# A sliding-window and a linear attention block in one kernel: six units fewer in the first superblock, and a new order of the filling work

## The chip, the cores and the metric

The kernel runs on one core of a Trainium2 chip. The metric is device time in microseconds (us) of one execution. Three runs of the kernel before gave 305.0, 306.4 and 856.78; their median is 306.4. A further execution was recorded by the hardware profiler; every duration of single instructions below is from it.

The core's engines work in parallel, each through its own instructions in order: TensorE (PE; its weight loads are shown as PEld), VectorE (DVE), ScalarE (ACT), GpSimd (POOL) and SyncE (SP, which here only issues transfers). Matrix products land in PSUM banks, from which VectorE or ScalarE must take them ("evacuate") before a bank can be used again.

## What is computed

Two independent attention blocks, A and B, each with its own input of 2048 rows by 640, 32 heads of width 20, an input projection (640 by 1920) and an output projection (640 by 640). Their results stand side by side in the output. All tensors are bf16.

```python
def A(x, wqkv, wo):                      # causal softmax attention in a window of 256
    q, k, v = heads_of(x @ wqkv)
    scores = einsum("bhqd,bhkd->bhqk", q, k) * 20 ** -0.5
    scores = where((i_q - i_k >= 0) & (i_q - i_k < 256), scores, -1e9)
    return merge(einsum("bhqk,bhkd->bhqd", softmax(scores), v)) @ wo

def B(x, wqkv, wo):                      # linear attention, not causal
    q, k, v = heads_of(x @ wqkv)
    phi = lambda t: where(t > 0, t + 1, exp(t)) + 1e-6
    kv = einsum("bhsd,bhse->bhde", phi(k), v)      # one 20 x 20 matrix a head
    z = einsum("bhsd->bhd", phi(k))
    num = einsum("bhqd,bhde->bhqe", phi(q), kv)
    return merge(num / (einsum("bhqd,bhd->bhq", phi(q), z)[..., None] + 1e-6)) @ wo
```

## The kernel before

**Superblocks, groups and units.** The 2048 rows are cut into four superblocks (`s`) of 512 rows, each of four blocks of 128. The 32 heads make eight groups (`g`) of four. For A, a query block meets its own key block (masked along the diagonal, kind "D"), the one before it (whole, "F") and the one before that (masked at the edge of the window, "E"). The table `TILES` lays these blocks for one superblock and group into three tiles, each four block columns wide; a tile of one group is a **unit**, so there are 4 x 8 x 3 = 96. Key blocks ahead of the first row don't exist, so in the first superblock the first tile has three block columns, the second two and the third four.

**One unit.** `scores` (L429) multiplies queries and keys of four heads at once into S_ps, which takes four PSUM banks and has a single buffer; ScalarE takes the exponential of the used columns into the tile p, of which there are three (L439); GpSimd masks the D and E blocks in p (`affine_select`, L455). Two units later (`LAG = 2`) `values` (L476) multiplies p with the values into O_ps, one PSUM bank with a single buffer. The values carry a column of ones, so the sum of the weights comes out beside them. After a group's third tile VectorE takes the reciprocal (L489) and the product (L490) into otok, a tile of one buffer, which four transposing transfers turn into oT for the output projection (L501).

**The filling work.** Everything else is one long sequence of generators, `fill`. Each yields the number of columns after every matrix product; the main loop emits a unit, then takes from `fill` until a credit of (`FILL` - `TAIL`) / units = 345680 / 96 = 3601 columns is used up. 17920 columns (`EARLY`) are taken ahead of the first unit, and some 22000 are left for the end. So the order of `fill` and the credit fix, in the program, what stands between two units on every engine. The parts of `fill`, all through a pool of three PSUM banks named dense (`dps`):

- `a_qk(s)` projects A's queries and keys, 25600 columns. VectorE evacuates into st (L165), and `bounce` writes st to scratch in memory (L198) and at once reads it back from there into qpad or kpad, heads apart (four transfers on SP's queue, L201).
- `a_v(s)`: A's values, 12800 columns (L173, evacuated at L165).
- `b_kv(s)`, 28800 columns: `tok_rows` projects B's keys, five chains, each followed by `phi` (ScalarE's exponential into e at L181 or L297, then two VectorE instructions at L182 or L298, the clamp, and L185 or L306); then `v_proj`, eight chains of values; then phi(k) times v into kv_acc (L320, L328, L330). In the last superblock kv_acc is multiplied with bd, a mask of ones where a row belongs to its own head, into kv_bd (L334). `build_masks` makes bd at the start.
- `b_q(s)`: phi of B's queries, five chains, 12800 columns.
- `b_num(s)`: eight halves, two to a block of rows; three products (L382), then on VectorE the sum + 1e-6 (L391), its reciprocal (L394) and the product (L395) into otokB, then a transposing transfer (L404). A half counts as 450 columns.
- `a_out(s)`, `b_out(s)`: the output projections, five chains each, evacuated into osb (L165); GpSimd issues the store (L282).
- `load`: a transposing transfer of 512 input rows into xA or xB (two buffers each), on SP's queue (L98).

`alt(a, b)` takes one yield of a, then five of b, in turn. The order before is

```python
fill = seq(a_qk(1), a_v(1), load("A", 2), b_kv(0), load("B", 2), b_kv(1), load("B", 3),
    a_qk(2), a_v(2), load("A", 3), a_out(0), b_kv(2), load("B", NS), b_kv(3), load("B", NS + 1),
    a_qk(3), a_v(3), b_q(0), load("B", NS + 2), alt(b_num(0), seq(a_out(1), b_q(1))), load("B", NS + 3),
    alt(b_num(1), seq(b_out(0), b_q(2))), alt(b_num(2), seq(b_out(1), b_q(3))),
    alt(b_num(3), a_out(2)), b_out(2), b_out(3))
```

Ahead of it stand `a_qk(0)`, the loads of B's first two superblocks and `a_v(0)`; behind it `a_out_last`, the last output projection of A. With the first unit `late_loads` issues three weight loads on GpSimd.

## Time and profile before

| what | us |
|---|---|
| median of three runs | 306.4 |
| the profiled execution | 306.14 |
| its span, first to last instruction | 304.4 |
| TensorE, matrix products busy | 275.2 |
| ScalarE busy | 193.8 |
| VectorE busy | 184.7 |
| GpSimd busy | 163.3 |
| exponentials of p (L439), 96 | 170.1 |
| masks of p (L455), 184 | 146.7 |

The first scores start at 33.83, the first exponential of p at 36.60, the last one at 283.47; the last evacuation begins at 301.2. So 37 us go before the units and 19 behind the last exponential. The granted TensorE clock is full throughout.

How to read the lines: in a timeline a line has the start and the length in us, the engine, the line of the kernel, the operation, output<-inputs with their shape, how often (x), and in brackets how long the engine had been idle before it and what released it. A list of groups has the busy time, the mean in ns, and the idle time ahead of the group. Matrix products are pipelined: one of 512 columns is shown as 0.38 long, but they start 0.21 apart.

### The profile page before, as it was taken

The page shows a single profiled execution, that of the slowest core. Times are in us where ns is not written, and L with a number is a line of the kernel's source. Part 1 is how long each engine was busy: PE and PEld are TensorE (multiplying, and loading weights), DVE is VectorE, ACT ScalarE, POOL GpSimd, SP SyncE. Part 2 cuts the span into 40 slices and gives each one's busy share as a digit, 9 for nine tenths or more (in the row PEclk, how much of TensorE's full clock was granted, in tenths as well). Part 3 has the DMA queues.
Part 4 walks back from the last instruction along what each step waited for, and adds up shares of the span by engine and source line. Part 5 has one row for each costly group of instructions (what it writes and reads, how often), then busy time and mean ns, then how long its engine had stood idle before and what let it go on. Part 6 is the DMA issues. An engine that isn't in the chain of part 4 may idle for free.

```text
span 304.4 us, 8052 instructions
## 1 busy us (share of the span) xinstructions
PE 275.2 (90%) x3440; PEld 156.8 (52%) x3440; DVE 184.7 (61%) x411; ACT 193.8 (64%) x143; POOL 163.3 (54%) x219
## 2 busy tenths in 40 slices
PE   3999799899899999989989999989888989989895
PEld 2355355564564565566556446545444545545562
DVE  1466345765664554566467545478668679678761
ACT  3000167757657777987876777887795895886202
POOL 7000096545454676856766567665564666656410
PEclk9999999999999999999999999999999999999999
DMA  7976999494040767701206445444436502502595
GB/s 245 295 269 163 176 278 299 109 167 76 2 78 13 172 158 109 170 2 24 64 3 88 88 127 135 88 47 87 129 67 147 140 0 45 131 0 45 85 216 177
DMA packets 66659, 35.91 MB, mean 118 GB/s; under 512 B 50784, under 2 KB 65248, under 8 KB 66624
## 3 DMA queue, kind: packets, MB, share of 16 engines
q1 hardware_dynamic: 63776, 27.04, 42.4%
q0 software_dynamic: 1536, 7.05, 6.8%
q10 hardware_dynamic: 1312, 1.31, 1.4%
q8 instruction: 27, 0.44, 0.6%
q14 instruction: 8, 0.07, 0.1%
HBM read 12.45 MB, written 10.49 MB: 75 GB/s over the span
## 4 chain that ended last, share of the span: by engine, by line
PE 44%; ACT 18%; DVE 15%; issue 12%; DMA 8%; SPq 1%; ACTq 0%; DVEq 0%
PE dense L173 28%; ACT p L439 14%; PE S_ps L429 8%; PE O_ps L476 6%; ACT e L181 4%; DMA k_scr<-st 3%; DVE phi L185 3%; DVE e L182 2%; DVE otokB L395 2%; DMA oT<-otok 2%; DMA kpad<-k_scr 2%; DVE otok L490 1%; DMA otok<-in_A_x_dram 1%; DVE denB L394 1%; DVE osb L165 1%
## 5 line engine op out<-in xcount | busy, mean ns | idle before, releaser
L439 ACT ACTIVATE p<-S_ps 128x2048 bf16<-128x2048 f32 (+2 forms) x96 | 170.1, 1772 | 88.0 <-PE S_ps L429 83.7
L455 POOL TENSOR_SCALAR_AFFINE_SELECT p<-p 128x512 bf16<-128x512 bf16 (+1 forms) x184 | 146.7, 819 | 124.1 <-ACT p L439 123.9
L476 PEld LDWEIGHTS <-p 128*128 128x128 bf16 x1440 | 42.7, 96 | 22.2 <-issue 14.8
L476 PE MATMUL O_ps<-vA,p 128*128 128x21 bf16 x1440 | 51.7, 173 | 2.6 <-DVE otok L490 1.8
L173 PE MATMUL dense<-wB,xB 128*128 128x320 bf16 (+2 forms) x320 | 49.4, 298 | 3.2 <-DVE phi L306 2.6
L173 PE MATMUL dense<-xA,wA 128*128 128x512 bf16 x200 | 48.2, 389 | 0.7 <-DVE xA L118 0.5
L165 DVE CAST st<-dense 128x512 bf16<-128x512 f32 x40 | 27.6, 691 | 25.1 <-PE dense L173 24.8
L429 PE MATMUL S_ps<-qpad,kpad 20*128 20x128 bf16 (+2 forms) x704 | 37.7, 275 | 5.4 <-DMA kpad<-k_scr 1.6
L182 DVE TENSOR_SCALAR e<-e 128x512 bf16<-128x512 bf16 x36 | 17.6, 488 | 30.5 <-ACT e L181 30.4
L429 PEld LDWEIGHTS <-kpad 20*128 20x128 bf16 x704 | 15.8, 92 | 36.6 <-issue 31.4
L173 PEld LDWEIGHTS <-xB 128*128 128x128 bf16 x320 | 26.1, 97 | 16.1 <-issue 4.5
L173 PEld LDWEIGHTS <-xA 128*128 128x128 bf16 x320 | 26.7, 97 | 14.6 <-issue 2.3
L165 DVE CAST osb<-dense 128x512 bf16<-128x512 f32 (+1 forms) x39 | 25.2, 647 | 13.4 <-PE dense L173 13.4
L173 PEld LDWEIGHTS <-wA 128*128 128x128 bf16 x200 | 18.7, 99 | 21.5 <-issue 3.3
L173 PE MATMUL dense<-woA,oT 128*128 128x512 bf16 (+1 forms) x160 | 26.1, 299 | 1.7 <-DVE phi L185 1.0
L173 PE MATMUL dense<-woB,xA 128*128 128x512 bf16 (+1 forms) x160 | 25.4, 299 | 1.7 <-DVE otokB L395 1.3
L173 PE MATMUL dense<-xB,wB 128*128 128x512 bf16 x100 | 25.0, 378 | 1.9 <-DVE otokB L395 1.5
L185 DVE SCALAR_TENSOR_TENSOR phi<-dense,e 128x512 bf16<-128x512 f32 x36 | 24.9, 692 | 1.2
L173 PE MATMUL dense<-wA,xA 128*128 128x320 bf16 x160 | 24.0, 299 | 0.0
L165 DVE CAST vA<-dense 128x320 bf16<-128x320 f32 x32 | 15.6, 493 | 12.0 <-PE dense L173 12.0
L181 ACT ACTIVATE e<-dense 128x512 bf16<-128x512 f32 x36 | 20.7, 601 | 0.7 <-PE dense L173 0.7
L165 DVE CAST vB<-dense 128x320 bf16<-128x320 f32 x32 | 15.1, 489 | 7.4 <-PE dense L173 7.1
(38 smaller groups left out, 148.1 us busy)
## 6 DMA issues: line engine op xcount, KB each, us to landing
out_dram<-osb POOLq DMA_DIRECT2D x7, 640.0 KB, 3.9
qpad<-q_scr SPq DMA_DIRECT2D x16, 160.0 KB
kpad<-k_scr SPq DMA_DIRECT2D x16, 160.0 KB
wA<-in_A_wqkv_dram SPq DMA_DIRECT2D x3, 800.0 KB
q_scr<-st SPq DMA_DIRECT2D x3, 640.0 KB
k_scr<-st SPq DMA_DIRECT2D x3, 640.0 KB
wB<-in_B_wqkv_dram SPq DMA_DIRECT2D x2, 800.0 KB
wB<-in_B_wqkv_dram POOLq DMA_DIRECT2D x1, 800.0 KB, 8.0
```

The costliest lines, as they stand in the source:

```text
L165: nc.vector.tensor_copy(out=dst, in_=src)
L173: nc.tensor.matmul(dst, lhsT=lhs(kt), rhs=rhs(kt), start=(kt == 0), stop=(kt == KT - 1))
L181: nc.scalar.activation(out=e[:], in_=src, func=ACT.Exp)
L182: nc.vector.tensor_scalar(out=e[:], in0=e[:], scalar1=1e-6, scalar2=1.0 + 1e-6, op0=ALU.add, op1=ALU.min)
L185: nc.vector.scalar_tensor_tensor(out=dst, in0=src, scalar=0.0, in1=e[:], op0=ALU.max, op1=ALU.add)
L394: nc.vector.reciprocal(out=den[:], in_=den[:])
L395: nc.vector.tensor_tensor(out=ot[:, tb, i * hh * DH : (i + 1) * hh * DH].rearrange("p (h e) -> p h e", e=DH), in0=ov[:, :, 0:DH], in1=den[ ...
L429: nc.tensor.matmul(S_ps[:, j, blk * P : blk * P + n], lhsT=kt[32 * j : 32 * j + DH, g, ko : ko + P], rhs=q_pad[s][32 * j : 32 * j + DH, g, ...
L439: nc.scalar.activation(out=p[:, :, lo:hi], in_=S_ps[:, :, lo:hi], func=ACT.Exp, scale=scale)
L455: nc.gpsimd.affine_select(out=v, in_=v, pattern=[[0, 4], [0, b1 - b0], [sgn, P]], compare_op=ALU.is_ge, fill=0.0, base=0 if kind == "D" el ...
L476: nc.tensor.matmul(O_ps[:, qb, j, :], lhsT=p[:, j, b * P : (b + 1) * P], rhs=v_tok[kb // TPS][:, kb % TPS, 4 * g + j, :], start=(t == 0 an ...
L490: nc.vector.tensor_tensor(out=otok_A[s][:, :, g * 4 * DH : (g + 1) * 4 * DH].rearrange("p t (h e) -> p t h e", e=DH), in0=O_ps[:, :, :, 0:DH],
```

## The change

Seven edits in one:

1. In the first superblock a group has two tiles of four block columns instead of three partly filled ones; the first query block of every group, which has only its diagonal block, goes into an extra wide tile ("X") for four groups together, with an O_ps of its own. That makes 2 + 16 = 18 units there and 90 in all, each with an exponential over 2048 columns. The credit of a unit becomes 345680 / 90 = 3841 columns. An X unit issues sixteen score products instead of eight, and one mask over all its four block columns.
2. `fill` has another order: `b_kv(2)` before `a_qk(2)`, `a_qk(3)` before `b_kv(3)`, and `a_v(3)` behind it, among the outputs.
3. A new `even` mixes two generators chain by chain (chains end in an `End`). In `b_kv` key chains and value chains take turns; `b_q(0)` and `b_num(0)` take turns with `a_v(3)` and `a_out(1)`; of each later output projection one chain stands in a `b_q` and four among the eight halves of a `b_num`.
4. The own-head mask is two `affine_select` on kv_bd in place, on GpSimd, in the last `b_kv`; bd and its making are gone, and the last sum goes into kv_bd directly.
5. otok becomes otokA, with two buffers.
6. The reads from scratch are issued later: those of the queries after the keys' write, those of the keys 25 products into the next generator (for the first superblock at once).
7. B's first two loads are issued between the two halves of `a_qk(1)`, behind its queries' write.

```diff
-TILES = [
-    [(0, 0, [(0, "D"), (1, "F"), (2, "E")]), (-2, 3, [(0, "E")])],
-    [(2, 0, [(2, "D"), (3, "F")]), (-1, 2, [(0, "F"), (1, "E")])],
-    [(3, 0, [(3, "D")]), (1, 1, [(1, "D"), (2, "F"), (3, "E")])],
-]
+def tiles_of(s):
+    out = []
+    for g in range(NG):
+        if s == 0:
+            if g % 4 == 0:
+                out.append(((s, g, "X"), True, True, [(g + i, 0, i, [(0, "D")]) for i in range(4)]))
+            tiles = [
+                [(g, 2, 0, [(2, "D"), (3, "F")]), (g, 0, 2, [(1, "F"), (2, "E")])],
+                [(g, 3, 0, [(3, "D")]), (g, 1, 1, [(1, "D"), (2, "F"), (3, "E")])],
+            ]
+        else:
+            tiles = [
+                [(g, 0, 0, [(0, "D"), (1, "F"), (2, "E")]), (g, -2, 3, [(0, "E")])],
+                [(g, 2, 0, [(2, "D"), (3, "F")]), (g, -1, 2, [(0, "F"), (1, "E")])],
+                [(g, 3, 0, [(3, "D")]), (g, 1, 1, [(1, "D"), (2, "F"), (3, "E")])],
+            ]
+        for t, parts in enumerate(tiles):
+            out.append(((s, g, "G"), t == 0, t == len(tiles) - 1, parts))
+    return out
...
     NHC = max(b - a + 1 for a, b in heads_of)
-    bd = wp.tile([P, KT, NHC, HV], BF16, name="bd")
...
+    def keep_own_head(t, c):
+        a, b = heads_of[c]
+        nh = b - a + 1
+        off = c * P - a * DH
+        v = t[:, c, 0:nh, :]
+        for sgn, base in ((1, off), (-1, DH - 1 - off)):
             nc.gpsimd.affine_select(
+                out=v,
+                in_=v,
+                pattern=[[-sgn * DH, nh], [0, HV]],
                 compare_op=ALU.is_ge,
                 fill=0.0,
+                base=base,
+                channel_multiplier=sgn,
             )
...
+    class End(int):
+        pass
+    def even(a, na, b, nb, lead=False):
+        def one(g):
+            for c in g:
+                yield c
+                if isinstance(c, End):
+                    break
+        done = 0
+        for i in range(na):
+            while lead and done < nb and done * na <= i * nb:
+                done += 1
+                yield from one(b)
+            yield from one(a)
+            while not lead and done * na < (i + 1) * nb:
+                done += 1
+                yield from one(b)
+        yield from a
...
     q_pad, k_pad, v_tok = {}, {}, {}
+    late_reads = {}
...
         sv = scratch.rearrange("(g j d) n -> j d g n", j=4, d=DH)
-        for j in range(4):
-            nc.sync.dma_start(out=dst[32 * j : 32 * j + DH, :, :], in_=sv[j])
-    def a_qk(s):
+        def reads():
+            for j in range(4):
+                nc.sync.dma_start(out=dst[32 * j : 32 * j + DH, :, :], in_=sv[j])
+        return reads
+    def a_qk(s, between=()):
         for n, base in (("q", 0), ("k", D)):
...
                 evac(st[:, c, :], ps[:])
-                yield SB
-            if n == "q":
-                q_pad[s] = qp.tile([P, NG, SB], BF16, name="qpad")
-                bounce(n, s, st, q_pad[s])
-            else:
-                k_pad[s] = kp.tile([P, NG, SB], BF16, name="kpad")
-                bounce(n, s, st, k_pad[s])
+                if c == KT - 1:
+                    pad, pl, name = (q_pad, qp, "qpad") if n == "q" else (k_pad, kp, "kpad")
+                    pad[s] = pl.tile([P, NG, SB], BF16, name=name)
+                    if n == "q":
+                        q_reads = bounce(n, s, st, pad[s])
+                        for g in between:
+                            yield from g
+                    else:
+                        late_reads[s] = bounce(n, s, st, pad[s])
+                        q_reads()
+                yield End(SB)
+    def hook(gen, n, fn):
+        for i, c in enumerate(gen):
+            if i == n:
+                fn()
+            yield c
...
-        yield from tok_rows(xB[s], w_sb["B"], D, done)
-        yield from v_proj("B", xB[s], vB)
+        rows = tok_rows(xB[s], w_sb["B"], D, done)
+        values_of = v_proj("B", xB[s], vB)
+        yield from even(rows, TPS + 1, values_of, TPS + 1)
+        yield from values_of
         for c in range(KT):
...
             else:
+                dst = kv_bd if s == NS - 1 else kv_acc
                 nc.vector.tensor_tensor(
-                    out=kv_acc[:, c, 0:nh, :], in0=pv, in1=kv_acc[:, c, 0:nh, :], op=ALU.add
+                    out=dst[:, c, 0:nh, :], in0=pv, in1=kv_acc[:, c, 0:nh, :], op=ALU.add
                 )
             if s == NS - 1:
-                nc.vector.tensor_tensor(
-                    out=kv_bd[:, c, 0:nh, :],
-                    in0=kv_acc[:, c, 0:nh, :],
-                    in1=bd[:, c, 0:nh, :],
-                    op=ALU.mult,
-                )
+                keep_own_head(kv_bd, c)
             yield TPS * P + P
...
-    def scores(s, g, t):
+    def scores(s, parts):
         S_ps = sps.tile([P, 4, SB], F32, name="S_ps")
         p = pp.tile([P, 4, SB], BF16, name="p")
-        parts = [x for x in TILES[t] if key(s, x[0]) >= 0]
-        for rel, blk, qs in parts:
+        for g, rel, blk, qs in parts:
             kb = key(s, rel)
...
                 )
-        lo = min(b for _, b, _ in parts) * P
-        hi = max(b + len(qs) for _, b, qs in parts) * P
-        nc.scalar.activation(
-            out=p[:, :, lo:hi], in_=S_ps[:, :, lo:hi], func=ACT.Exp, scale=scale
-        )
+        nc.scalar.activation(out=p[:], in_=S_ps[:], func=ACT.Exp, scale=scale)
...
-        return p, parts
-    def values(s, g, t, p, parts):
-        if t == 0:
-            O_of[s, g] = ops.tile([P, TPS, 4, HV], F32, name="O_ps")
-        O_ps = O_of[s, g]
+        return p
+    def values(okey, first, last, parts, p):
+        s, g, form = okey
+        if first:
+            O_of[okey] = ops.tile([P, TPS, 4, HV], F32, name="O_ps")
+        O_ps = O_of[okey]
         todo = []
-        for rel, blk, qs in parts:
+        for gg, rel, blk, qs in parts:
             for i, (qb, _) in enumerate(qs):
                 for j in range(4):
-                    todo.append((key(s, rel), blk + i, qb, j))
-        for n, (kb, b, qb, j) in enumerate(todo):
+                    todo.append((gg, key(s, rel), blk + i, gg - g if form == "X" else qb, j))
+        for n, (gg, kb, b, slot, j) in enumerate(todo):
             nc.tensor.matmul(
...
-        if t < 2:
+        if not last:
             return
-        if g == 0:
-            otok_A[s] = op1.tile([P, TPS, D], BF16, name="otok")
+        if s not in otok_A:
+            otok_A[s] = op.tile([P, TPS, D], BF16, name="otokA")
         r = sp.tile([P, TPS, 4, 1], F32, name="recA")
-        nc.vector.reciprocal(out=r[:], in_=O_ps[:, :, :, DH:HV])
+        w = 4 * DH
+        if form == "X":
+            t0, n = 0, 4
+            dst = otok_A[s][:, 0, g * w : (g + 4) * w].rearrange("p (t h e) -> p t h e", e=DH, h=4)
+        else:
+            t0 = 1 if s == 0 else 0
+            n = TPS - t0
+            dst = otok_A[s][:, t0:TPS, g * w : (g + 1) * w].rearrange("p t (h e) -> p t h e", e=DH)
+            O_ps = O_ps[:, t0:TPS, :, :]
+        nc.vector.reciprocal(out=r[:, 0:n, :, :], in_=O_ps[:, :, :, DH:HV])
         nc.vector.tensor_tensor(
-            out=otok_A[s][:, :, g * 4 * DH : (g + 1) * 4 * DH].rearrange(
-                "p t (h e) -> p t h e", e=DH
-            ),
+            out=dst,
             in0=O_ps[:, :, :, 0:DH],
-            in1=r[:].to_broadcast([P, TPS, 4, DH]),
+            in1=r[:, 0:n, :, :].to_broadcast([P, n, 4, DH]),
             op=ALU.mult,
         )
+        if form == "X":
+            return
         if g == NG - 1:
...
     run(a_qk(0))
-    run(seq(load("B", 0), load("B", 1)))
+    late_reads[0]()
     run(a_v(0))
+    def k_reads(s, gen):
+        return hook(gen, 25, lambda: late_reads[s]())
+    outs = seq(a_v(3), a_out(1), b_out(0), b_out(1), a_out(2))
     fill = seq(
-        a_qk(1),
-        a_v(1),
+        a_qk(1, between=(load("B", 0), load("B", 1))),
+        k_reads(1, a_v(1)),
         load("A", 2),
...
         load("B", 3),
+        b_kv(2),
+        load("B", NS),
         a_qk(2),
-        a_v(2),
+        k_reads(2, a_v(2)),
         load("A", 3),
         a_out(0),
-        b_kv(2),
-        load("B", NS),
-        b_kv(3),
+        a_qk(3),
+        k_reads(3, b_kv(3)),
         load("B", NS + 1),
-        a_qk(3),
-        a_v(3),
-        b_q(0),
-        load("B", NS + 2),
-        alt(b_num(0), seq(a_out(1), b_q(1))),
+        even(seq(b_q(0), load("B", NS + 2), b_num(0)), 3 * TPS + 1, outs, 3 * TPS + 1, lead=True),
+        even(b_q(1), KT, outs, 1),
         load("B", NS + 3),
-        alt(b_num(1), seq(b_out(0), b_q(2))),
-        alt(b_num(2), seq(b_out(1), b_q(3))),
-        alt(b_num(3), a_out(2)),
+        even(b_num(1), 2 * TPS, outs, 4, lead=True),
+        even(b_q(2), KT, outs, 1),
+        even(b_num(2), 2 * TPS, outs, 4, lead=True),
+        even(b_q(3), KT, outs, 1),
+        even(b_num(3), 2 * TPS, outs, 4, lead=True),
+        outs,
         b_out(2),
...
     take(EARLY)
-    units = [(s, g, t) for s in range(NS) for g in range(NG) for t in range(3)]
+    units = [u for s in range(NS) for u in tiles_of(s)]
     LAG = 2
...
     credit = 0.0
-    for s, g, t in units:
-        p, parts = scores(s, g, t)
-        if (s, g, t) == (0, 0, 0):
+    for i, (okey, first, last, parts) in enumerate(units):
+        p = scores(okey[0], parts)
+        if i == 0:
             late_loads()
-        pend.append((s, g, t, p, parts))
+        pend.append((okey, first, last, parts, p))
         if len(pend) > LAG:
...
         credit += rate
```

The scores and values of a unit, the division and the tail are otherwise as before; `End` replaces the plain number at the end of each chain.

More of the change, by code (lines that the diff above doesn't have):

```diff
@@ L101, in load_x_first @@
     def load_x_first():
-        tok = op1.tile([P, TPS, D], BF16, name="otok")
+        tok = op.tile([P, TPS, D], BF16, name="otokA")
         src = xsrc["A"][0:SB, :].rearrange("(t p) d -> p t d", p=P)
@@ L128 @@
     NHC = max(b - a + 1 for a, b in heads_of)
-    bd = wp.tile([P, KT, NHC, HV], BF16, name="bd")
-    def build_masks():
-        nc.gpsimd.memset(bd[:], 1.0)
-        for c in range(KT):
-            a, b = heads_of[c]
-            nh = b - a + 1
-            off = c * P - a * DH
+    def keep_own_head(t, c):
[4 more added lines that the diff above has]
+        for sgn, base in ((1, off), (-1, DH - 1 - off)):
             nc.gpsimd.affine_select(
-                out=bd[:, c, 0:nh, :],
-                in_=bd[:, c, 0:nh, :],
-                pattern=[[-DH, nh], [0, HV]],
+                out=v,
+                in_=v,
+                pattern=[[-sgn * DH, nh], [0, HV]],
                 compare_op=ALU.is_ge,
                 fill=0.0,
-                base=off,
-                channel_multiplier=1,
-            )
-            nc.gpsimd.affine_select(
-                out=bd[:, c, 0:nh, :],
-                in_=bd[:, c, 0:nh, :],
-                pattern=[[DH, nh], [0, HV]],
-                compare_op=ALU.is_ge,
-                fill=0.0,
-                base=DH - 1 - off,
-                channel_multiplier=-1,
+                base=base,
+                channel_multiplier=sgn,
             )
@@ L237, in v_proj @@
                 )
-                yield hh * DH
+                yield End(hh * DH)
     def a_v(s):
@@ L255, in tok_rows @@
             done(tb, ps)
-            yield SB
+            yield End(SB)
         ps = bank()
@@ L268, in tok_rows @@
         done(None, pv)
-        yield P
+        yield End(P)
     def wo_proj(n, oT, s, col0):
@@ L369, in b_q @@
             phi(pq[:, c, :], ps[:])
-            yield SB
+            yield End(SB)
     def b_num(s):
@@ L402, in b_num @@
                 )
-                yield 3 * 150
+                yield End(3 * 150)
             nc.sync.dma_start_transpose(
@@ L436, in scores @@
                 )
-        lo = min(b for _, b, _ in parts) * P
-        hi = max(b + len(qs) for _, b, qs in parts) * P
-        nc.scalar.activation(
-            out=p[:, :, lo:hi], in_=S_ps[:, :, lo:hi], func=ACT.Exp, scale=scale
-        )
+        nc.scalar.activation(out=p[:], in_=S_ps[:], func=ACT.Exp, scale=scale)
         runs = []
-        for rel, blk, qs in sorted(parts, key=lambda x: x[1]):
+        for _, _, blk, qs in sorted(parts, key=lambda x: x[2]):
             for i, (_, kind) in enumerate(qs):
@@ L473, in values @@
                 for j in range(4):
-                    todo.append((key(s, rel), blk + i, qb, j))
-        for n, (kb, b, qb, j) in enumerate(todo):
+                    todo.append((gg, key(s, rel), blk + i, gg - g if form == "X" else qb, j))
+        for n, (gg, kb, b, slot, j) in enumerate(todo):
             nc.tensor.matmul(
-                O_ps[:, qb, j, :],
+                O_ps[:, slot, j, :],
                 lhsT=p[:, j, b * P : (b + 1) * P],
-                rhs=v_tok[kb // TPS][:, kb % TPS, 4 * g + j, :],
-                start=(t == 0 and n == 0),
-                stop=(t == 2 and n == len(todo) - 1),
+                rhs=v_tok[kb // TPS][:, kb % TPS, 4 * gg + j, :],
+                start=(first and n == 0),
+                stop=(last and n == len(todo) - 1),
@@ L538, in seq @@
             yield from g
-    def alt(a, b):
-        live = [(a, 1), (b, KT)]
-        while live:
-            for g in list(live):
-                for _ in range(g[1]):
-                    try:
-                        yield next(g[0])
-                    except StopIteration:
-                        live.remove(g)
-                        break
     xA[0], transposes = load_x_first()
@@ L558 @@
     transposes()
-    build_masks()
     def late_loads():
```

## The prediction, made before the changed kernel ran

> **What bounds the kernel now.** I read the page's first part, then the chain of work that ended last, because a busy share says nothing of order.
>
> ```profile
> PE 275.2 (90%) x3440; PEld 156.8 (52%) x3440; DVE 184.7 (61%) x411; ACT 193.8 (64%) x143; POOL 163.3 (54%) x219
> ...
> PE 44%; ACT 18%; DVE 15%; issue 12%; DMA 8%; SPq 1%; ACTq 0%; DVEq 0%
> ```
>
> TensorE looks full, yet ScalarE and VectorE hold a third of the chain. The timeline of a quiet stretch tells why:
>
> ```profile
> 106.33 0.40 PE L429 MATMUL S_ps<-qpad,kpad 20*128 20x128 bf16 x8
> ...
> 106.67 0.56 PE L476 MATMUL O_ps<-vA,p 128*128 128x21 bf16 x16
> 106.86 1.88 ACT L439 ACTIVATE p<-S_ps 128x2048 bf16<-128x2048 f32 x1 [0.58 <-PE S_ps L429]
> ...
> 107.08 1.65 PE L173 MATMUL dense<-wA,xA 128*128 128x320 bf16 x11
> ...
> 108.79 0.40 PE L429 MATMUL S_ps<-qpad,kpad 20*128 20x384 bf16 x8
> ```
>
> S_ps has one buffer. The exponential starts at 106.86 and ends at 108.74; only then (108.79) may the next scores be written, and 0.53 later the next exponential starts. This **cycle of 2.46** (1.88 + 0.58 idle) is exact from 97 to 124. TensorE's own work in a unit: 0.33 until the values start, 0.42 for 16 value products, 0.214 per 512-column product (five in 1.07, from 104.63 to 105.70), 0.14 per 320 columns. Seven products of 512 make 2.25, so about 0.2 is left over. Where a unit is longer, a stall is behind it. The waits by line:
>
> ```profile
> PE dense L173 <- DVE otokB L395: 3.5, 6, 1.0
> PE dense L173 <- DVE phi L306: 2.6, 4, 1.3
> PE dense L173 <- DVE phi L185: 1.9, 5, 0.7
> ...
> PE S_ps L429 <- ACT p L439: 1.4, 5, 0.3
> ```
>
> (us in total, times, longest.) TensorE waits for one of the three dense banks. In the timeline at 215:
>
> ```profile
> 215.22 0.82 PE L173 MATMUL dense<-xB,wB 128*128 128x512 bf16 x3 [0.97 <-DVE otokB L395]
> ...
> 216.51 1.88 ACT L439 ACTIVATE p<-S_ps 128x2048 bf16<-128x2048 f32 x1 [1.78 <-PE S_ps L429]
> ```
>
> The stall on B's division makes the next scores late, ScalarE idles 1.78 instead of 0.58, and nothing recovers it.
>
> For each of the 95 intervals between exponentials (36.60 to 283.47, 246.9 in all) I took the larger of its exponential + 0.575 and its TensorE work, counted from the products issued in it. The sum is 54.0 + 58.9 + 58.9 + 56.5 = 228.3 by superblock. The other **18.6 are stalls**: 7.4 in the four b_kv stretches, 9.2 in the four b_num stretches, 0.7 in b_q(0), 0.9 in the other b_q, 0.4 elsewhere.
>
> **The change, part by part.** All against the profiled execution, 306.1 (span 304.4 and 1.7 around it); the median, 306.4, is nearly the same.
>
> *18 units for 24.* The forms of the exponential:
>
> ```profile
> L439 ACT ACTIVATE p<-S_ps 128x1536 bf16<-128x1536 f32 x8 | 11.6, 1453 | 31.7 <-PE S_ps L429 31.6
> L439 ACT ACTIVATE p<-S_ps 128x1024 bf16<-128x1024 f32 x8 | 8.2, 1026 | 5.0 <-PE S_ps L429 5.0
> ```
>
> With eight of 1.88 these are 34.8; 18 full ones are 33.8. ScalarE gains 1.0 only; what goes is six gaps. Value products stay 1440, and fill columns stay, so each unit carries 3841 of them instead of 3601. By the same rule the changed order gives 44.5 + 59.1 + 59.1 + 56.6 = 219.3 over 89 intervals: **-9.0**. TensorE's mean rises from 2.24 to 2.36, so this holds only while it still fits under 2.46; 40 units need 2.40 or more, where five did. Late scores there cost between 0 and 40 x 0.05 = 2; I take **+0.4**, as those five lost nearly nothing.
>
> *The wide unit.* Twice a unit has sixteen score products for eight; eight weight loads of S_ps take 0.25, so eight more add some 0.25 each time. Its select over 2048 elements isn't in the trace; 512 take 0.69 and 1024 take 1.11, hence 1.95 as an estimate. POOL then issues three weight loads (39.39 to 42.14: 2.75) before it masks unit 1 (1.32), so those values are due at 43.7 and ready at 44.4. Both together **+1.2** (0 to 2).
>
> *b_kv: rows alternate with values.* A phi's exponential queues behind the running p, then VectorE needs about 1.2, so its bank comes free 1.85 after the next unit's scores start; the value chain two chains later wants that bank. Walking the new order chain by chain: in b_kv(0) two value chains find it taken, 0.9 each, cost 1.8; in b_kv(1) short ones, 0.5. Mean 1.15, four times 4.6, against 7.4: **-2.8**. Ends: no stall (-7.4), or 1.1 in each of 20 pairs (22 - 7.4 = +14.6); I stay at the walk. b_q(0) now alternates with a_v(3) likewise: 1.5 for 0.7, **+0.8** (-0.7 to +6). In exchange nearly every unit has one phi exponential at most (0.60, in the 0.58 gap), where pairs took the unit to 2.73.
>
> *Division.* A half of b_num costs VectorE 0.166 + 0.253 + 0.492 = 0.91, 1.0 with gaps, and TensorE 0.18; an output evacuation 0.69. b_num(0) meets a chain per half and fits (2.2 to 2.7 a unit). b_num(1) to (3) meet four chains per eight halves: VectorE gets 14.3, 12.9 and 11.0 in 4, 4 and 3 units, 4.5, 3.1 and 3.6 more than the cycles. Three banks hide about 1.5 of each; with 1 for b_num(0) some 8, against 9.2: **-1.2** (4 to 12.2, the latter with no bank hiding). The other b_q: **+0.3** (0 to 1).
>
> *B's keys and values forward.* b_kv(2) goes ahead of a_qk(2), and a_qk(3) ahead of b_kv(3). At 3841 columns a unit a_qk(2) ends at unit 34, its k reads are issued at 37, and superblock 2 begins at unit 42; a_v(3) ends at 62 for values at 68. Nothing waits: 0; if a read came late, its 5.7 would be due against five units, 12.3.
>
> *Own-head mask.* Five multiplies (2.5) leave VectorE; ten selects of 0.375 join POOL at b_kv(3). Cost nothing: values lag two units; without that cover up to 1.2. *Two row buffers*: VectorE's otok idled 1.1 in all, none for a transfer: 0.
>
> *Transfers.* At the start xB's transposes leave the way of the k reads. Those reads' packets ended 6.0 after issue (29.49), and 5.7 after issue at 189.35, undisturbed: **-0.1** (0 to -0.4). xB is issued about 2 later, needed at 48. But SP's queue now holds k write, q reads, k reads, then A's rows for superblock 3, and those are due 25,600 columns after the k write: 6.7 units, 16.4. Rows say 6.2 (k write at 109.79 to reads at 115.96) + 1.5 + 8.2 (rows issued 117.49, landed 125.7) = 15.9. **+0.5** (0 to 7.4, if the k write takes the 13.6 of the one at 45.25). The tail keeps its 22,000 columns: 0.
>
> *A rule against the change.* The phi clamp waits for a running select:
>
> ```profile
> 126.28 1.96 POOL L455 TENSOR_SCALAR_AFFINE_SELECT p<-p 128x512 bf16<-128x512 bf16 x2
> ...
> 126.47 1.93 DVE L182 TENSOR_SCALAR e<-e 128x512 bf16<-128x512 bf16 x1 [2.41 <-ACT e L181]
> ```
>
> It takes 0.28 alone. The second wide select falls among b_kv(0)'s phis and could hold a bank 1.2 longer. The Trainium skill ("GPSIMD Engine Reference", Specifications) says GpSimd shares its SBUF interfaces with VectorE and contends with two-port instructions. Taken as certain, that would make the sum 1.2 worse; by the row it is one clamp's luck, and I add nothing.
>
> Sum: -9.0 + 0.4 + 1.2 - 2.8 + 0.8 - 1.2 + 0.3 - 0.1 + 0.5 = **-9.9**, so 306.1 - 9.9 = **296.2**.
>
> **Rivals.**
> 1. *VectorE is the bound of the last superblock.* No bank hides a deficit (12.2 for 8: +4.2) and b_kv gains nothing (+2.8): 303.2. For it: VectorE is busy 8.9 and 9.1 of 10 in 230:240 and 250:260. Against: at 240:250 only 6.2, so there is room to catch up.
> 2. *A's rows come late* behind the scratch reads: +7.4, 303.6. That part then doesn't do what it says: it moves a wait. Against: SP idles most of that time.
> 3. *Slower: alternation blocks banks.* Place: the 26 pairs of phi and value chain. If each pays the 0.9 of the two in my walk: 23.4 for the 6.1 charged, +17.3, 313.5. The gain is gone from 0.62 a pair, and it is over 2% slower from 0.86. For it: TensorE's slack falls to 0.1. Against: the phase of the chains drifts, and b_kv(1) in the walk pays little.
>
> **How the numbers follow.** Forecast 0.65, rival 1 0.21, rival 2 0.06, rival 3 0.08. A measurement can tell about 2% from no change: 300.3 to 312.5. Faster 0.65, same 0.27, slower 0.08. Low end: b_kv without stalls (-4.6) and the wide unit for nothing (-1.2) give 290.4. High end: rivals 1 and 2 lie inside 304.5; rival 3 stays out.
>
> **What would show it.** 90 exponentials, all 2048 wide; 18 in some 48 us after a start at 36.5; 2.46 in quiet stretches; the last one near 274; a phi exponential alone between two p; bank waits on otokB remaining. It is wrong if quiet units run at 2.55 or more (TensorE then is the bound), or if values of B wait 0.9 for phi's bank again and again.

## The result

Four runs of the changed kernel gave a median of 301.82 us (301.41 to 302.72); the kernel before, in the runs taken with it, 306.12. The ratio is 0.9876 with a 95% interval of [0.9835, 0.9916]: about 1.2% faster. The profiled execution took 301.41 with a span of 299.6, against 306.14 and 304.4. So **-4.7 came where -9.9 was forecast**, inside the range and with the right sign, and less than half of it. The ratio is of fast runs alone, without the 856.78 of the kernel before.

### The profile page after: what moved, and what is told of

Its sections match the earlier page's. It is cut to its first block, busy times and chain, and to the rows that moved or that the text cites. A ratio compares the mean times of both kernels' runs of the same rounds, so it can differ in the third digit from the quotient of the medians.

```text
span 299.6 us, 8085 instructions
## 1 busy us (share of the span) xinstructions
PE 273.3 (91%) x3472; PEld 155.1 (52%) x3472; DVE 184.4 (62%) x410; ACT 193.3 (65%) x137; POOL 161.0 (54%) x212
## 4 chain that ended last, share of the span: by engine, by line
PE 47%; DVE 16%; DMA 11%; ACT 10%; issue 9%; POOL 5%; SPq 1%; ACTq 0%; DVEq 0%
PE dense L179 32%; ACT p L480 7%; PE O_ps L516 6%; PE S_ps L472 6%; DMA xA<-in_A_x_dram 4%; DMA k_scr<-st 4%; ACT e L187 3%; DVE phi L191 3%; DVE e L188 3%; POOL p L494 3%; DVE otokB L439 2%; DVE osb L171 2%; DMA kpad<-k_scr 2%; DMA otokA<-in_A_x_dram 1%; DVE denB L438 1%
## 5 line engine op out<-in xcount | busy, mean ns | idle before, releaser
L480 ACT ACTIVATE p<-S_ps 128x2048 bf16<-128x2048 f32 x90 | 169.0, 1877 | 83.4 <-PE S_ps L472 78.0
L494 POOL TENSOR_SCALAR_AFFINE_SELECT p<-p 128x512 bf16<-128x512 bf16 (+2 forms) x178 | 144.9, 837 | 122.7 <-ACT p L480 122.6
L188 DVE TENSOR_SCALAR e<-e 128x512 bf16<-128x512 bf16 x36 | 20.3, 564 | 35.1 <-ACT e L187 35.1
L472 PE MATMUL S_ps<-qpad,kpad 20*128 20x256 bf16 (+2 forms) x736 | 36.3, 270 | 2.9 <-DMA kpad<-k_scr 1.3
L472 PEld LDWEIGHTS <-kpad 20*128 20x128 bf16 x736 | 13.5, 92 | 32.7 <-issue 28.9
L179 PE MATMUL dense<-xB,wB 128*128 128x512 bf16 x100 | 25.7, 378 | 1.3 <-DVE osb L171 1.1
L179 PE MATMUL dense<-woB,xA 128*128 128x512 bf16 (+1 forms) x160 | 24.9, 298 | 2.0 <-DVE osb L171 2.0
L179 PE MATMUL dense<-wA,xA 128*128 128x320 bf16 x160 | 25.0, 299 | 0.8 <-DVE otokB L439 0.6
L191 DVE SCALAR_TENSOR_TENSOR phi<-dense,e 128x512 bf16<-128x512 f32 x36 | 24.9, 692 | 1.2
L179 PE MATMUL dense<-woA,oT 128*128 128x512 bf16 (+1 forms) x160 | 24.8, 299 | 0.3 <-DVE osb L171 0.3
L539 DVE TENSOR_TENSOR otokA<-O_ps,recA 128x320 bf16<-128x320 f32 (+1 forms) x34 | 16.0, 472 | 1.4 <-DVE recA L538 0.3
```

The source lines that it names most:

```text
L179: nc.tensor.matmul(dst, lhsT=lhs(kt), rhs=rhs(kt), start=(kt == 0), stop=(kt == KT - 1))
L188: nc.vector.tensor_scalar(out=e[:], in0=e[:], scalar1=1e-6, scalar2=1.0 + 1e-6, op0=ALU.add, op1=ALU.min)
L191: nc.vector.scalar_tensor_tensor(out=dst, in0=src, scalar=0.0, in1=e[:], op0=ALU.max, op1=ALU.add)
L472: nc.tensor.matmul(S_ps[:, j, blk * P : blk * P + n], lhsT=kt[32 * j : 32 * j + DH, g, ko : ko + P], rhs=q_pad[s][32 * j : 32 * j + DH, g, ...
L480: nc.scalar.activation(out=p[:], in_=S_ps[:], func=ACT.Exp, scale=scale)
L494: nc.gpsimd.affine_select(out=v, in_=v, pattern=[[0, 4], [0, b1 - b0], [sgn, P]], compare_op=ALU.is_ge, fill=0.0, base=0 if kind == "D" el ...
```

## The profile after

First the page of the changed kernel: busy time by engine, and the shares of the chain of work that ended last.

```profile
PE 273.3 (91%) x3472; PEld 155.1 (52%) x3472; DVE 184.4 (62%) x410; ACT 193.3 (65%) x137; POOL 161.0 (54%) x212
...
PE 47%; DVE 16%; DMA 11%; ACT 10%; issue 9%; POOL 5%; SPq 1%; ACTq 0%; DVEq 0%
```

No engine became much busier. In the chain ScalarE fell from 18% to 10%, and **DMA rose from 8% to 11%**: a transfer now holds up work that it did not hold before. The groups of the two instructions that matter most (busy time and mean ns, then the idle time ahead of them):

```profile
L480 ACT ACTIVATE p<-S_ps 128x2048 bf16<-128x2048 f32 x90 | 169.0, 1877 | 83.4 <-PE S_ps L472 78.0 <-POOL p L494 3.6 <-POOL kv_bd L152 0.6
...
L188 DVE TENSOR_SCALAR e<-e 128x512 bf16<-128x512 bf16 x36 | 20.3, 564 | 35.1 <-ACT e L187 35.1
```

90 exponentials, all full: that step happened as written. The clamp of phi takes 564 ns in the mean where it took 488.

The quiet stretches do not all keep the cycle of 2.46. ScalarE's exponentials in `a_qk(3)`:

```profile
151.23 1.88 ACT L480 ACTIVATE p<-S_ps 128x2048 bf16<-128x2048 f32 x1 [0.58 <-PE S_ps L472]
153.80 1.88 ACT L480 ACTIVATE p<-S_ps 128x2048 bf16<-128x2048 f32 x1 [0.69 <-PE S_ps L472]
156.26 1.88 ACT L480 ACTIVATE p<-S_ps 128x2048 bf16<-128x2048 f32 x1 [0.58 <-PE S_ps L472]
```

A unit with seven 512-column products takes 2.46 (153.80 to 156.26), one with eight 2.57 (151.23 to 153.80): ScalarE idles 0.69 instead of 0.58 because the scores come later. The two alternate, since 3841 columns are seven and a half such products. There are ten units of the longer kind, 1.1 in all.

The same sum as in the prediction (each interval between two exponentials against the larger of exponential + 0.575 and its TensorE work; what is over is a stall) for the changed kernel:

| us | before | after | forecast of the difference | measured |
|---|---|---|---|---|
| first exponential | 36.60 | 36.26 | -0.1 | -0.3 |
| intervals without stalls | 228.3 | 219.3 | -9.0 | -9.0 |
| stalls in b_kv, four stretches | 7.4 | 6.2 | -2.8 | -1.2 |
| in b_q(0) with a_v(3) | 0.7 | 1.1 | +0.8 | +0.5 |
| in b_num, four stretches | 9.2 | 10.0 | -1.2 | +0.8 |
| in the other b_q | 0.9 | 2.2 | +0.3 | +1.2 |
| in a_qk(3), with A's late rows | 0 | 2.7 | +0.5 | +2.7 |
| elsewhere (wide unit, late scores) | 0.4 | 1.1 | +1.6 | +0.7 |
| from last exponential to the end | 22.67 | 22.54 | 0 | -0.1 |

The gain that was computed is there to a tenth. It went back as stalls, 18.6 before and 23.3 after, where a fall to 17.8 had been forecast. Which waits these are, in the list of waits (us in total, times, longest) of the changed kernel:

```profile
PE dense L179 <- DVE osb L171: 3.3, 8, 0.7
PE dense L179 <- DVE phi L191: 2.4, 6, 0.8
PE dense L426 <- DVE phi L191: 2.1, 4, 0.7
PE dense L179 <- DMA xA<-in_A_x_dram: 2.1, 1, 2.1
```

The waits on the division (otokB) are no longer at the top, but waits on output evacuations and on phi for the same three banks are. The last line is new: one wait of 2.1 on A's input rows.

**b_kv(0) in the timeline**, where the prediction's walk had put two stalls of 0.9:

```profile
60.54 1.45 PE L179 MATMUL dense<-wB,xB 128*128 128x320 bf16 x16 [0.77 <-DVE phi L191]
...
61.13 2.01 POOL L494 TENSOR_SCALAR_AFFINE_SELECT p<-p 128x2048 bf16<-128x2048 bf16 x1 [0.83 <-ACT p L480]
61.58 1.71 DVE L188 TENSOR_SCALAR e<-e 128x512 bf16<-128x512 bf16 x1 [0.69 <-ACT e L187]
...
62.45 1.88 ACT L480 ACTIVATE p<-S_ps 128x2048 bf16<-128x2048 f32 x1 [0.91 <-PE S_ps L472]
...
63.32 0.69 DVE L191 SCALAR_TENSOR_TENSOR phi<-dense,e 128x512 bf16<-128x512 f32 x1
...
64.06 1.38 PE L179 MATMUL dense<-wB,xB 128*128 128x320 bf16 x9 [0.73 <-DVE phi L191]
...
65.91 1.88 ACT L480 ACTIVATE p<-S_ps 128x2048 bf16<-128x2048 f32 x1 [1.09 <-PE S_ps L472]
```

Both stalls are there (0.82 and 0.95 over the ideal). The second shows what the prediction had weighed and set at nothing: the wide select runs from 61.13 to 63.14, the clamp beside it takes 1.71 instead of 0.3, phi ends at 64.01, and the value chain gets its bank 0.73 late.

**b_num(1)**, where one unit took 4.28 (the exponential before began at 224.73):

```profile
224.67 0.37 DVE L188 TENSOR_SCALAR e<-e 128x512 bf16<-128x512 bf16 x1 [0.92 <-ACT e L187]
...
225.82 0.33 PE L426 MATMUL dense<-kv_bd,phi 128*128 128x84 bf16 x3 [0.72 <-DVE phi L191]
...
226.42 1.24 PE L179 MATMUL dense<-woB,xA 128*128 128x512 bf16 x5 [0.27 <-DVE osb L171]
...
227.66 0.49 DVE L439 TENSOR_TENSOR otokB<-dense,denB 128x320 bf16<-128x320 f32 x1
...
228.21 0.34 PE L426 MATMUL dense<-kv_bd,phi 128*128 128x84 bf16 x3 [0.39 <-DVE otokB L439]
...
229.01 1.88 ACT L480 ACTIVATE p<-S_ps 128x2048 bf16<-128x2048 f32 x1 [2.40 <-PE S_ps L472]
```

Three halves and an output chain stand in that one unit. TensorE waits for a bank three times, 0.72, 0.27 and 0.39, and the scores come 1.8 late. VectorE works through all three waits; ahead of them, up to the clamp at 224.67, it had idled 0.92 for ScalarE's exponential. The same holds wherever TensorE waits for a dense bank between 195 and 285 (18 waits, 8.1 in all): VectorE is at work in every one.

**A's rows for superblock 3.** First SyncE's own view of its queue, then TensorE's timeline, both of the changed kernel:

```profile
128.38 0.38 SPq L229 DMA_DIRECT2D k_scr<-st  x1
128.85 2.42 SPq L234 DMA_DIRECT2D qpad<-q_scr  x4
132.83 1.48 SPq L234 DMA_DIRECT2D kpad<-k_scr  x4
134.36 8.77 SPq L113 DMA_TRANSPOSE xA<-in_A_x_dram  x1
```

```profile
144.16 0.38 PE L179 MATMUL dense<-woA,oT 128*128 128x128 bf16 x4
146.64 1.67 PE L179 MATMUL dense<-xA,wA 128*128 128x512 bf16 x7 [2.10 <-DMA xA<-in_A_x_dram]
```

From the k write to the issue of the rows 6.0 passed (estimated 6.2 + 1.5), but the issue of their load took 8.77, and 12.3 passed from its start to the first use, where the estimate had 8.2. They were due at 144.5 and came at 146.6. In the kernel before, the same load stood behind the k reads alone, and in the 1.5 ahead of it the transfer engines were busy 19% of the time. Here the q reads were issued just before the k reads, and in the 1.6 ahead of the load (132.8 to 134.4) the share is 69%. That these reads made the issue long is argued from the shares; no run left them out.

## The experiments

Two theories for the stalls stood against each other. **F**: fuller units. With 3841 columns a cycle instead of 3601, each unit carries more chains, thus more turns of the three banks, and a late bank finds no slack left. **V**: VectorE's work in the last superblock is the bound, and the new order only shifts it. The late rows were tested by themselves.

### Tiles alone, and the whole change with single parts undone

*e1*: the kernel before with the new tiles and units only; the order of `fill`, the loads, the own-head mask and the single otok stay as before.

```diff
...
-    units = [(s, g, t) for s in range(NS) for g in range(NG) for t in range(3)]
+    units = [u for s in range(NS) for u in tiles_of(s)]
...
```

> The kernel before with edit 1 alone (90 units instead of 96; order, loads, mask and buffers as before). Theory S (cycles and stalls are separate terms): the six cycles bring their 9.0, the stalls stay at 18.6 plus some 2 for fuller units and the wide unit, so 306.1 - 7 = 299 (298 to 300.5), faster than the whole change (301.8). Theory F (what six fewer units save, the fuller units lose again in any order): 301 to 303, like the whole change.

Measured: 302.47, ratio 0.9918 [0.9887, 0.9949]. The intervals without stalls are 219.0, and the stalls 24.9; about 2.1 of these lie beside a window of half clock at the first units (told below), so some 22.8. **The fuller units alone raised the stalls by about 4.2**: b_kv 7.4 to 9.0 (0.7 of it beside the second wide unit), b_num 9.2 to 9.5, the other b_q 0.9 to 2.7, and some 0.6 in quiet units. Without any of the new order the kernel ran as fast, within the intervals, as with all of it (0.9876, and 0.9882 in a second set of runs, e11 below).

*e2*: the change, with A's rows for superblock 3 loaded ahead of `a_qk(2)`.

```diff
         load("B", NS),
+        load("A", 3),
         a_qk(2),
         k_reads(2, a_v(2)),
-        load("A", 3),
         a_out(0),
```

> The changed kernel, with the load of A's rows for superblock 3 issued ahead of a_qk(2) instead of behind the k reads. If the 2.1 that TensorE waits for these rows are lost for good: 301.8 - 2.2 = 299.6 (299.2 to 300.2), and the interval of 4.83 at unit 41 becomes 2.46. If the wait is covered elsewhere, or the earlier load delays another transfer: 301.5 to 302.

Measured: 299.22, ratio 0.9798 [0.9761, 0.9836]. SyncE's view and TensorE's timeline of this kernel:

```profile
110.48 2.95 SPq L113 DMA_TRANSPOSE xA<-in_A_x_dram  x1
```

```profile
143.93 0.38 PE L179 MATMUL dense<-xA,wA 128*128 128x512 bf16 x1
```

The load is issued 17.5 before the k write, its issue takes 2.95 instead of 8.77, and a_qk(3) starts without a wait. The stall of a_qk(3) falls from 2.70 to 0.64; every other stretch keeps its stalls to 0.02. So the moved load cost 2.06, as a wait for a transfer, and this is settled. Half of the 0.64 left is in the units of eight products.

*e3*: the change, with key chains first and value chains behind them in `b_kv`.

```diff
-        yield from even(rows, TPS + 1, values_of, TPS + 1)
+        yield from rows
         yield from values_of
```

> The changed kernel with b_kv as before (five key chains, then eight value chains), everything else changed. If taking turns saves stalls, as in the prediction's walk (6.2 lost now, 7.4 before): 303 (302.3 to 304). If taking turns blocks banks: 300 (299.5 to 301).

Measured: 303.72, 0.9950 [0.9921, 0.9979]. b_kv has 7.3 instead of 6.2. So alternation does gain, 1.15. The 1.7 from there to e1's 9.0 belongs to other parts of the new order, which no run took apart. The time itself says less: all twelve executions of e3 have a mean granted clock of 0.994 or less, and six of ten of the change.

*e4*: the change without the sum + 1e-6 in B's division, so one VectorE instruction less in each half (that part of the computation is left out).

```diff
-                nc.vector.tensor_scalar_add(
-                    out=den[:], in0=ov[:, :, DH:HV], scalar1=1e-6
-                )
-                nc.vector.reciprocal(out=den[:], in_=den[:])
+                nc.vector.reciprocal(out=den[:], in_=ov[:, :, DH:HV])
```

> The changed kernel without the addition of 1e-6 to B's denominators, which is left out: 32 VectorE instructions of 0.17, with their gaps 6.4 us. If VectorE is the bound of the b_num stretches, the 10.0 lost there shrink by 1.6 for each of the three tight ones and 0.5 for the first: 301.8 - 5 = 297 (296 to 298.5). If the stalls there come from waiting times of single banks or from TensorE, at most a third of it: 300.2 to 301.8.

Measured: 300.93, 0.9847 [0.980, 0.9894], which can't be told from the change. VectorE had 4.8 less to do. In b_num(0), (1) and (3) the stalls fell by 0.3, 0.6 and 0.8; b_num(2) lay in a window of half clock and can't be compared. Were VectorE's total the bound, each would have lost about as much as VectorE saved, 8 x 0.166 = 1.3. It was a fifth to three fifths of that, so VectorE's work is a part of the cause.

### What fills a unit

*e5*: the change with only three of five products in each chain of b_out(0), b_out(1) and a_out(2) (the output projections there are incomplete); chains, evacuations and credit as before.

```diff
...
-        yield from wo_proj("B", oT_B[s], s, D)
+        yield from wo_proj("B", oT_B[s], s, D, 3 if s in (0, 1) else KT)
...
```

> The changed kernel with three of five products in the chains of b_out(0), b_out(1) and a_out(2), which leaves two fifths of these sums out: TensorE has 0.43 less in each of 12 chains and 0.44 less in three, 6.5 in all, VectorE the same work in the same order. Theory V (VectorE and the banks it holds set the b_num stretches): their 10.0 of stalls, counted against the cycle, stay within 1 of it, b_q's 2.2 shrink by up to 1: 300 to 302. Theory T (TensorE's full units turn every wait into time): half of the 12.2 goes: 295 to 297.

Measured, one run: 301.77 (before beside it 305.11). TensorE had some 6 less to do, and the stalls in b_num are 10.3 against 10.0, of which b_num(1), beside 6.8 of half clock, had 0.9 more than in the change. **Less TensorE work in these units removed little:** away from that window 0.8 of 8.9 in b_num and the other b_q.

*e6*: the change with the evacuations of the same three output projections on ScalarE.

```diff
...
-                evac(osb[:, tb, 0:SB], ps[:])
+                evac(osb[:, tb, 0:SB], ps[:], to)
...
-        yield from wo_proj("B", oT_B[s], s, D)
+        yield from wo_proj("B", oT_B[s], s, D, "A" if s in (0, 1) else None)
...
```

> The changed kernel with the evacuations of b_out(0), b_out(1) and a_out(2) on ScalarE (0.60 each) instead of VectorE (0.69). Theory V: VectorE loses 2.9 of work in each of three b_num stretches, their stalls halve: -3, 299 (298 to 300). Against it: an evacuation queued behind a running exponential holds its bank for up to 2 more, and two in one gap put 0.3 on the cycle: 302 to 304.

Measured: 303.07, 0.9925 [0.9886, 0.9965]. VectorE fell by 8.1, and the stalls are no less in sum: b_num 9.7, the other b_q 3.1 (10.0 and 2.2 in the change). TensorE now waits 1.8 for ScalarE's evacuations where it had waited 3.3 for VectorE's, and 4.8 for the division where it had waited 2.0. Why the division's waits grew is open.

*e7*: e2 with the halves of the last superblock spread wider: each of the first three `b_num` is mixed with a whole `b_q` and five chains of output, the last with five chains of output alone.

```diff
...
-        even(b_q(1), KT, outs, 1),
...
         load("B", NS + 3),
-        even(b_num(1), 2 * TPS, outs, 4, lead=True),
-        even(b_q(2), KT, outs, 1),
...
+        even(b_num(1), 2 * TPS, mix(b_q(2), outs), 2 * KT, lead=True),
...
```

> The changed kernel with the early rows, and the halves of b_num(s) spread over b_q(s+1) and four output chains instead of over four output chains alone (eight halves to nine chains). VectorE's work is then nearly even, 2.5 a unit. Theory V: b_num and b_q lose 7 instead of 12.2, 301.8 - 2.2 - 5 = 294.6 (293.5 to 297). If phi's queueing behind the exponential and the halves' chains add up instead: 299 to 301, no better than the early rows alone.

Measured: 305.02, 0.9986 [0.9933, 1.0039]. The mixed stretches have 17.1 of stalls where the change has 12.2 for the same work. TensorE's timeline shows the kind of wait (3.4 of half clock follow it, so the sum is somewhat too high):

```profile
226.05 1.24 PE L179 MATMUL dense<-woB,xA 128*128 128x512 bf16 x5
229.29 0.33 PE L426 MATMUL dense<-kv_bd,phi 128*128 128x84 bf16 x3 [2.01 <-DVE phi L191]
```

A half waits 2.01 for a bank that phi holds; VectorE works in 1.54 of it and first waits for ScalarE's exponential. The spreading did not make VectorE's load even: from one exponential to the next it is busy between 0.8 and 3.9 in the mixed stretch. So e7 shows a worse order and does not test theory V. **V as the whole cause is not borne out** by e4, where the stalls fell by a part of the work saved, nor by e6, though there ScalarE had the work instead.

*e8*: the change with lighter units, 3641 columns each; 18,000 columns more go behind the last unit.

```diff
-TAIL = 22000
+TAIL = 40000
```

> The changed kernel with 18000 columns of the filling work moved from the units to the end (TAIL 40000 for 22000): 3641 columns a unit, about as before the change. The end grows by 18000 / 2400 = 7.5. Theory F (fuller units turn short bank waits into time): stalls of b_kv, b_q and b_num fall by 3 to 4 of 19.5, to 16: 305 to 306. Theory S (stalls don't depend on the slack): they stay, less what falls out of the units: 308 to 309.

Measured, one run: 315.6; that time says little about the units, since the work behind them waits 2.25 and 3.78 for transposes and has 10.2 of half clock. In the stretches that lie within the units in both kernels the stalls fall from 14.9 to 10.9: b_kv 6.2 to 4.75, b_num(0) to (2) 7.6 to 5.5, b_q(1) and (2) 1.1 to 0.65.

*e9*: the kernel before with nothing of the change, but 3830 columns a unit.

```diff
-TAIL = 22000
+TAIL = 0
```

> The kernel before with TAIL 0 for 22000: nothing of the change, but 3830 columns a unit instead of 3601, as many as the change gives them. Theory F (the fuller unit alone turns short bank waits into time): the stalls rise from 18.6 to 22 or 23, the last exponential stays where it was or comes later (283 to 288), though nothing was added. Theory S (stalls are set by the order): they stay at 18.6 to 19.5, and the last exponential stays at 283 to 284.

Measured, one run: 312.16; the end is bare, with a wait of 4.82 for transposes and 10.2 of half clock. Within the units, the list of waits of this kernel and of the kernel before:

```profile
ACT p L439 <- PE S_ps L429: 90.8, 71, 27.8
```

```profile
ACT p L439 <- PE S_ps L429: 83.7, 73, 29.0
```

Leaving out the longest wait, the one ahead of the first unit, ScalarE waits 63.0 for scores against 54.7. By intervals the stalls are 24.2 against 18.6, 1 to 1.6 of it beside a window of half clock. e1, e8 and e9 agree on **F: some 4 of stalls come and go with the fullness of the units alone.** The total agrees, the places don't: e1's rise lies in b_kv and the other b_q, e9's in b_num (9.2 to some 12), while its b_kv fell by about 0.5. In b_num, by e5, it is hardly TensorE's time in the chains; that it is their number, each with a bank to be emptied, is argued.

*e12*: the change with three of five products in the chains of `b_kv` (B's keys and values are incomplete).

```diff
...
-        rows = tok_rows(xB[s], w_sb["B"], D, done)
-        values_of = v_proj("B", xB[s], vB)
+        rows = tok_rows(xB[s], w_sb["B"], D, done, 3)
+        values_of = v_proj("B", xB[s], vB, 3)
...
```

> The changed kernel with three of five products in the key and value chains of b_kv, which leaves two fifths of B's keys and values out: TensorE has 0.43 less a key chain and 0.28 less a value chain, 17 in the four stretches, while VectorE and ScalarE have the same work in the same order. Theory V (a bank that waits for phi, not TensorE's fullness, makes the stalls): b_kv's 6.2 stay between 5 and 7, the last exponential at 278 to 280. Theory T (TensorE is full there): they fall under 3, the last exponential to 275 or 276.

Measured, one run: 298.78 (before beside it 305.34). TensorE had 15 less to do; b_kv(1) to (3) fall from 4.1 to 2.2 though 3.4 of half clock lies in b_kv(2); b_kv(0), beside 6.8 of half clock, rises from 2.1 to 2.7. So in `b_kv` TensorE's time has a part in the stalls, and a larger one than in `b_num`; the size lies between what the two theories had expected, and the split stays open.

### Putting it together

*e10*: e2, with e4's edit (the 1e-6 is left out) and 3072 columns more ahead of the first unit.

```diff
-EARLY = 17920
-FILL = 367680
+EARLY = 20992
+FILL = 364608
...
```

> The changed kernel with the early rows, without the addition of 1e-6 to B's denominators (left out), and with 3072 columns more ahead of the first unit, where TensorE waits 1.3 for the k reads. Terms seen so far: -2.2 for the rows, -1.7 for the addition, -0.3 for the filled wait: 297.6 where the change alone is 301.8 (296.5 to 298.5). If the stalls behind the addition move on instead: 299.

Measured: 298.84, 0.9774 [0.973, 0.9819]. That can't be told from e2's 0.9798: b_num fell to 8.4, and b_kv rose to 7.95, presumably as its chains met the exponentials at other moments. So **e2 is the better version**: the whole computation, at 0.9798 of the kernel before.

*e11*: the change once more, beside e10.

> The changed kernel itself, beside the others on the same chip. Its ratio to the kernel before was 0.988; against the tiles alone (0.992) it should be within 0.5% either way, if the new order saves in b_kv what the late rows cost.

Measured: 302.48, 0.9882 [0.9831, 0.9934]. Stalls in b_kv, b_q and b_num repeat to 0.03. One stretch does not, a_qk(3) with 4.0 for 2.7, and the table by windows of time shows why (columns: window, its length, busy time and count of PE, PEld, DVE, ACT, POOL, granted TensorE clock, DMA share, GB/s). First this run, then the same window of the first execution of the change:

```profile
145.50:148.90 3.40, 2.68 (x7) 0.84 (x6) 0.35 (x1) 0.00 (x0) 2.42 (x3) 0.50 0.22 67
```

```profile
145.50:148.90 3.40, 2.26 (x28) 1.03 (x28) 0.69 (x1) 0.45 (x2) 2.45 (x3) 1.00 0.24 55
```

TensorE ran at half its clock for 3.4, beginning within the wait for A's rows; ScalarE got no scores in that time.

## Why the prediction was right and wrong

**Right.** Six cycles less: 228.3 to 219.3, -9.0 to the tenth; this is a count by the same rule and prices on both sides. The start and the tail came within 0.2 of what was said, and the stretch with the own-head mask, b_kv(3), has the smallest stalls of the four (0.7). The wide select took 2.01 for an estimated 1.95. The walk through b_kv(0) named the two units that stall. Their price came out too, the second by luck: 0.73 of its 0.95 is the wait for the phi that the wide select held up, which the walk did not count.

**Half right.** The prediction called itself wrong "if quiet units run at 2.55 or more (TensorE then is the bound)". Those of seven products stay at 2.46; those of eight run at 2.57, so there TensorE is the bound.

**Wrong, in order of size** (the whole miss is 5.2):

1. *"Late scores there cost between 0 and 2; I take +0.4, as those five lost nearly nothing."* This is the step that failed. It asked what a full unit costs where nothing else happens, and even that came to 1.1. It did not ask what a full unit does to a stretch that already stalls: the 18.6 had been counted at 3601 columns, and the fuller units alone took them to about 22.8 (e1), +4.2 where +0.4 stood. The walk through b_kv and the estimate for the divisions did look at the new units and were too low as well: 4.6 for 6.2 (b_kv(1) has 1.5 where the walk had 0.5), and 8 for 10.0. That b_kv has 2.8 less than in e1 (9.0 to 6.2), just the term forecast for alternating, is luck: alternating by itself gives 1.15 (e3). The other b_q (+1.2 for +0.3) and part of b_num belong here; 0.8 of that b_q lies in one unit that also has two halves of b_num(2).
2. *A's late rows, "+0.5 (0 to 7.4)".* The mechanism was stated, and its size was off: 2.06 (e2). The term that failed is the 8.2 from issue to landing. It came from a load that stood behind four reads; the change puts eight there, as the prediction itself listed, and it was over 12.
3. *Division, -1.2.* Measured +0.8, and +0.5 against e1. "Three banks hide about 1.5 of each" treated VectorE's deficit as the price, with a 1.5 that no run shows. By e4 the load explains only a part (a fifth to three fifths). VectorE is at work in every wait, so the moment at which its work comes matters; what seems to be left is latency: a division waits on VectorE behind a clamp that waits on ScalarE behind a running exponential, while the bank is held. The clamp at 224.67 is such a case; no run took that order apart, so it is argued and not shown.

Rival 1 (303.2) lay nearer in time than the forecast, and in part for another reason: of its +4.2 for VectorE's deficit 2.0 came, and e4 puts only a part of that down to VectorE. Rival 2 is what happened, at a quarter of its price. Rival 3's mechanism exists (b_kv(0)), at well below its 0.62 a pair.

**The rule weighed against the change.** The Trainium skill ("GPSIMD Engine Reference", Specifications) says that GpSimd shares its SBUF interfaces with VectorE. The prediction let the row decide and added nothing. The second wide select did fall on b_kv(0)'s clamp, 1.71 beside it, and TensorE then waited 0.73 for that phi; over the kernel the clamp's mean rose by 76 ns, 36 times, 2.7 on VectorE. With the key chains first (e3) that mean is 479, so it is the alternation that puts clamps beside selects. The rule pointed the right way: 0.73 of waiting where it would have added 1.2.

## What to carry to other kernels

When a change packs the same work into fewer cycles, count again the stalls that are there already: they aren't a constant. Here they grew from 18.6 to some 22.8 when a unit got 3841 columns for 3601. When a load is moved behind other transfers of one queue, take its time from issue to landing from a row with as many transfers ahead of it. And run the main part of a change alone: here it gave the whole gain within the intervals, and the rest showed only when one load was moved (e2, 0.9798).

## What the runs showed of the hardware

The granted TensorE clock fell to 0.50 for 3.4, sometimes 6.8 or 10.2, in stretches where TensorE had waited. A mean granted clock of 0.994 over an execution is one such window (3.4 x 0.5 / 300 = 0.006). Of ten executions of the change six had a mean of 0.994 or less; of twelve of e2 and e10, which lack the 2.1 wait for A's rows, none had. So the wait cost more than its length. It isn't the only occasion: ten of the twelve executions of e1, which lacks that wait, have a mean of 0.994 or less, and its profile has 6.8 of half clock at the first units. A window cost 1.3 in a_qk(3) (2.70 to 4.01) and 0.95 in b_num(2) (e3, 2.74 to 3.69).

The Trainium skill ("TensorE: Matmul & The Clock Gate", Part 1) describes a free-running activity window of 3413 ns and half rate after an idle one; the length agrees with the 3.4 seen. Its section "Why this matters for your kernels" asks only for no idle gap above about 3 us. Here a gap of 2.10 brought a window in some executions and not in others (e11, where 1.4 of it had passed when the window began), and in the 3.4 ahead of each of four windows TensorE idled 1.25 (e3, in three gaps), 1.4 (e11), 2.0 (e7) and 2.2 (e4). So the measured limit is lower than the page's.

The kept traces show the free running too. In each of them every start and end of half clock lies a whole number of steps of 3.413 from the first record of the clock, and that grid stands elsewhere in each execution. Taking TensorE's idle time in each step at full clock, over all 14 traces: half clock followed all 8 steps with 2.0 or more, 12 of 39 with 1.1 to 2.0, and none of 917 with less. The wait of 2.10 falls into one step with 1.36 and one with 0.75 in e11, which got a window, and into 0.81 and 1.29 in the first execution of the change, which got none. Idle time alone does not decide between 1.1 and 2.0, and some traces lack a few matrix products, so the bounds are rough.
